# Agents' weights read from PSUM, top-k words and ranks kept in a PSUM bank, key maxima taken in PSUM by halves

## The chip, the cores and the metric

The kernel runs on one core of a Trainium2 chip. The metric is the device time of one execution in microseconds; lower is better. Three runs of the kernel before gave 364.14, 364.25 and 367.25 us, median 364.25.

The names of the engines in the rows are PE (TensorE's matmuls), PEld (its weight loads), DVE (VectorE), ACT (ScalarE), POOL (GpSimd) and SP (the engine that issues most DMAs).

## What is computed

Agent attention over 4 batches of 12608 tokens with 128 channels and 49 agents, and behind it an expert of one hidden layer for the 128 tokens of each batch that score highest.

```python
def sm(a, b):
    s = scale * (a @ b.transpose(0, 2, 1))
    s = s - s.max(-1, keepdims=True)
    e = np.exp(s)
    return e / (e.sum(-1, keepdims=True) + 1e-09)
agent_v = sm(agents, k) @ v
x = sm(q, agents) @ agent_v
...
scores = np.einsum('bsd,d->bs', x, w_gate)
out = x.copy()
for b in range(B):
    top_idx = np.argpartition(-scores[b], capacity)[:capacity]
    xe = x[b, top_idx]
    ye = np.maximum(xe @ w1, 0.0) @ w2
    g = 1.0 / (1.0 + np.exp(-scores[b, top_idx]))
    out[b, top_idx] = x[b, top_idx] + g[:, None] * ye
```

## The kernel before

Each batch is cut into 7 chunks, six of 15 tiles of 128 tokens and one of 9. Queries and keys arrive transposed, one DMA of 960 KB a chunk (576 KB for the short one), values in another; five buffers in SBUF take turns for all of them and, later, for the output.

**Scores** (`scores`, L205). For one chunk of keys or queries TensorE makes two halves, of 32 agents each. A half is four matmuls that put 32 partitions each into one PSUM bank `S`; four tokens' columns lie side by side over the 128 partitions. There are two such banks (`psS`, shared with a part of the output matmuls at the end). VectorE transposes each half in 32 x 32 blocks into SBUF (L220), so that tokens lie on partitions, with the tile and the agent along the row.

**Key side.** `k_front` (L229) takes, after both halves, the maximum over the chunk's tiles for each agent (L238, a strided reduction of 735 elements to 49). `k_max` (L242) reduces over chunks, then over partitions by a transpose on TensorE, and spreads the 49 maxima over all partitions by a matmul with a diagonal. POOL subtracts them (L264), ScalarE takes the exponent (L267), and TensorE accumulates with the values into the bank `av` (L282).

**Agents' weights** (`v_finish`, L290). A matmul adds the two halves of `av` into `pw` in PSUM. VectorE divides by the sum of exponents (L302), takes each agent's product with the gate's weights as a further column (L303), finds a power of two that scales the whole into range (`iv`, L312 and L315), scales (L320), and splits the scaled 129 columns into a 16-bit high part `ws[:, 0]` (L323) and low part `ws[:, 1]` (L324).

**Query side.** Scores, maxima (L340), subtraction on POOL (L347), exponent on ScalarE (L348), and a split into two 16-bit parts (L368, L373), which TensorE transposes (L392). The gate's scores `pg` come from 396 matmuls of three columns (L407), which need `ws`, the outputs `po` from 792 (L448). Most of the outputs are made after all input is loaded, in the order of batches 0, 1, 3, 2; ScalarE, VectorE and POOL bring them to SBUF (L455 to L467), POOL multiplying for batches 3 and 2, and SP stores them.

**Top-k** (`topk`, L506). For each batch the 128 x 99 gate scores become integer words that sort like the numbers (L518 to L530). `radix` (L478) finds the word that bounds the top 128 in two searches of 8 rounds, on the high and then on the low half-word. In a round VectorE compares all words with three bounds (L489), TensorE counts (L494), VectorE sums (L496) and moves the bound (L500). Then ranks are made by prefix sums (L549 to L559), and two matmuls (L569) turn ranks into a list of tokens. The counts, the high half-words and the counting matmuls use a bank of PSUM: `R` for batches 0, 1 and 2, which therefore take turns (a list, `counting`, also keeps the program text in that order), and `V` for batch 3. A search's words lie in SBUF.

**Experts** (`expert`, L616). POOL gathers the 128 rows by an indirect DMA (L633), queries for batches 0 to 2, which are then attended anew (`attend`), stored outputs for batch 3. TensorE transposes them (`qT`, L642) and makes the hidden layer (`ph`, L664) and the result (`py`, L676); POOL scatters it over the stored outputs (L686). The last two scatters end the kernel.

**What sets the order.** The program is written as generators that are advanced beside the main loop, with priorities (TOPK, RANK, CHASE, GATES and others). A scheduler then lays the instructions of each engine in one fixed order, by dependencies, priorities and its own estimates of durations. Each engine runs its row in that order, so an instruction that waits holds up all that stand behind it.

## Time and profile before

| | |
|---|---|
| runs | 364.14, 364.25, 367.25 us |
| profiled execution | 367.46 us, its span from first to last instruction 365.2 us |
| busy share of the span | PE 84%, DVE 79%, POOL 50%, ACT 46% |
| granted TensorE clock, mean | 0.932 |
| HBM | 79.83 MB read, 26.21 MB written |
| chain of waits, by engine | PE 52%, DVE 32%, POOL 5%, issue 4%, DMA 4%, ACT 2% |

Spans are read from the first instruction. A busy share is a mean over stretches with different limits; which engine limits a stretch is read from the table of stretches and from the idle times in the timelines. An entry of a timeline may hold several instructions of one line (x8), with the duration of all. Matmuls of fp32 data appear twice in it, once for each pass.

### The profile page before, as it was taken

Reading aid. Unit: us, or ns where it says so; the run is one execution under the profiler, and the core shown is the slowest. Engines: PE = TensorE matmul, PEld = TensorE weight load, DVE = VectorE, ACT = ScalarE, POOL = GpSimd, SP = SyncE. Lnnn points to the kernel's source line nnn. Section 1 sums busy time; section 2 is a strip of 40 time slices with the busy share of each in tenths; the row PEclk is TensorE's granted clock in tenths of the full one; section 3 lists DMA queues with packets and bytes.
Section 4 is the critical chain, followed back from the end, with each engine's and each line's share of the span. In section 5 each row is a group of like instructions: output and inputs, shape, how many; then the busy total and the mean of one; then the engine's idle time right before and its main releaser. Section 6 shows DMA issues by size and latency. Waiting matters only on the chain.

```text
span 365.2 us, 9066 instructions
## 1 busy us (share of the span) xinstructions
PE 308.0 (84%) x3669; PEld 199.9 (55%) x3669; DVE 287.6 (79%) x761; ACT 169.6 (46%) x293; POOL 182.9 (50%) x149
## 2 busy tenths in 40 slices
...
GB/s 298 408 420 415 346 281 391 228 304 334 420 377 132 367 359 336 347 385 141 396 337 308 403 354 178 157 189 222 2 263 293 351 286 209 305 355 257 133 375 16
DMA packets 18586, 106.63 MB, mean 292 GB/s; under 512 B 2544, under 2 KB 3952, under 8 KB 18544
## 3 DMA queue, kind: packets, MB, share of 16 engines
...
q8 instruction: 29, 0.48, 0.5%
q0 software_dynamic: 256, 0.52, 0.4%
...
HBM read 79.83 MB, written 26.21 MB: 290 GB/s over the span
## 4 chain that ended last, share of the span: by engine, by line
PE 52%; DVE 32%; POOL 5%; issue 4%; DMA 4%; ACT 2%; POOLq 0%; ACTq 0%; DVEq 0%
PE S L213 17%; PE po L448 10%; PE av L282 9%; PE fT L392 6%; DVE mx L238 6%; DVE sk L220 5%; DVE sq L220 3%; PE pg L407 3%; DVE qm L340 2%; PE bk L494 2%; DMA cst<-consts 2%; DVE qm L351 2%; POOL sq L347 2%; DMA out<-og 1%; POOL f L373 1%
## 5 line engine op out<-in xcount | busy, mean ns | idle before, releaser
L213 PE MATMUL S<-xT,ag_sb 128*32 128x480 f32 (+1 forms) x896 | 117.0, 586 | 15.2 <-DMA ag_sb<-agT 6.3
L393 ACT COPY ft<-fT 98x896 f16<-98x896 f16 (+2 forms) x49 | 42.7, 899 | 58.4 <-PE fT L392 58.2
L448 PE MATMUL po<-ws,ft 98*128 98x128 f16 x792 | 63.7, 235 | 5.8 <-DVE ws L323 2.2
L347 POOL TENSOR_TENSOR sq<-sq,qm 128x735 f32<-128x735 f32 (+1 forms) x28 | 38.2, 1369 | 56.6 <-DVE qm L340 52.3
L448 PEld LDWEIGHTS <-ft 98*128 98x128 f16 x792 | 54.8, 107 | 14.2 <-issue 13.4
L282 PE MATMUL av<-v,sk 128*64 128x129 f32 x792 | 60.9, 291 | 0.6 <-ACT sk L267 0.6
L213 PEld LDWEIGHTS S<-xT,ag_sb 128*32 128x32 f32 x896 | 24.9, 113 | 61.5 <-issue 16.8
L282 PEld LDWEIGHTS av<-v,sk 128*64 128x64 f32 x792 | 50.2, 144 | 11.5 <-issue 7.5
L373 POOL TENSOR_TENSOR f<-sq,f 128x735 f16<-128x735 f32 (+1 forms) x28 | 41.2, 1476 | 28.7 <-ACT f L368 23.7
L264 POOL TENSOR_TENSOR sk<-sk,mb 128x735 f32<-128x735 f32 (+1 forms) x28 | 46.7, 1712 | 10.0 <-DVE mb L257 10.0
L220 DVE STREAM_TRANSPOSE sk<-S 128x480 f32<-128x480 f32 (+1 forms) x56 | 35.0, 640 | 12.0 <-PE S L213 11.2
L348 ACT ACTIVATE sq<-sq,lift 128x735 f32<-128x735 f32 (+1 forms) x28 | 24.8, 887 | 41.0 <-POOL sq L347 40.8
L392 PEld LDWEIGHTS <-f 128*98 128x98 f16 x396 | 26.9, 127 | 23.0 <-issue 16.4
L238 DVE TENSOR_REDUCE mx<-sk 128x49 f32<-128x735 f32 (+1 forms) x28 | 38.9, 1390 | 0.3
L392 PE MATMUL fT<-idh,f 128*98 128x128 f16 x396 | 34.1, 227 | 5.4 <-POOL f L373 4.5
L220 DVE STREAM_TRANSPOSE sq<-S 128x480 f32<-128x480 f32 (+1 forms) x56 | 34.7, 636 | 5.0 <-PE S L213 4.7
L368 ACT CAST f<-sq 128x735 f16<-128x735 f32 (+1 forms) x28 | 22.0, 789 | 31.2 <-POOL sq L362 24.5
L362 POOL TENSOR_TENSOR sq<-sq,qm 128x735 f32<-128x735 f32 (+1 forms) x14 | 19.1, 1367 | 31.7 <-DVE qm L355 28.2
L467 POOL TENSOR_TENSOR og<-og,r 128x512 f32<-128x512 f32 (+2 forms) x33 | 30.3, 946 | 7.6 <-ACT og L466 5.0
L496 DVE TENSOR_REDUCE bk<-bk 128x3 f32<-128x99 f32 x64 | 16.5, 259 | 21.1 <-PE bk L494 20.6
L457 ACT ACTIVATE og<-po,iv 128x512 f32<-128x512 f32 (+1 forms) x35 | 22.3, 669 | 20.6 <-PE po L448 13.4
L267 ACT ACTIVATE sk<-sk 128x735 f32<-128x735 f32 (+1 forms) x28 | 22.1, 797 | 18.7 <-POOL sk L264 18.2
...
## 6 DMA issues: line engine op xcount, KB each, us to landing
...
```

The source lines that it names most:

```text
L213: nc.tensor.matmul(ps[32 * i:32 * i + 32, :w], ag_sb[:, b, 32 * h:32 * h + 32], xt[:, w * i:w * i + w], start=True, stop=True,)
L220: nc.vector.transpose(dst[:, :n, 32 * h:32 * h + 32], ps[:, :w].rearrange("p (t c) -> p t c", c=32),)
L238: nc.vector.tensor_reduce(d["mx"][:, c], s[:, :n, :A].rearrange("p t a -> p a t"), axis=AX.X, op=ALU.max)
L264: nc.gpsimd.tensor_tensor(sv, sv, st[b]["mb"].unsqueeze(1).broadcast_to([P, n, A]), op=ALU.subtract)
L282: nc.tensor.matmul(d["av"][o:o + AP_, :C + 1], d["S"][c][:, t], d["v", c][:, t], start=(j < 2), stop=(j >= COLS - 2),)
L347: nc.gpsimd.tensor_tensor(sv, sv, m[:, :n].unsqueeze(2).broadcast_to([P, n, A]), op=ALU.subtract)
L348: nc.scalar.activation(sv, sv, AF.Exp, scale=SCALE, bias=lift)
L373: nc.gpsimd.tensor_tensor(f[:, :n, A:], st[b]["q", c][:, :n, :A], f[:, :n, :A], op=ALU.subtract)
L392: nc.tensor.transpose(pt[:2 * A, P * t:P * t + P], f[:, t0 + t, :], idh)
L393: (nc.vector.tensor_copy if TURN[b][t0 // 8] == "V" else nc.scalar.copy)(d["ft", c][:2 * A, P * t0:P * (t0 + nt)], pt[:2 * A, :P * nt])
L448: nc.tensor.matmul(p3[:, t], q_tile(b, c, t0 + t), d["W"][:, i, :C], start=(i == 0), stop=(i == 1))
L467: nc.gpsimd.tensor_tensor(o4, o4, rate.broadcast_to([P, nt, C]), op=ALU.mult)
```

## The change

Three parts. *Key maxima*: the reduction moves into `scores`. Right after each half's transpose VectorE reduces the same PSUM bank along its row, 480 elements to 1, one maximum for each of the 128 partitions; `k_max` then works on 2 columns instead of 49. *Agents' weights*: the high and low parts are made from `pw` in PSUM by one operation each, with the reciprocal sum and the scale as per-partition factors; the 129th column and the factors' product go to ScalarE (four small operations) and POOL (one subtraction). *Top-k*: the scores are first copied into the search's PSUM bank, and the words, half-words, comparisons and ranks are written there, at four places (0, KEYS, SUMS, FREE) that are used again in turn; ScalarE copies two constants that VectorE copied or read before.

```diff
-    def scores(src, b, c, dst):
+    def scores(src, b, c, dst, top=None):
...
             nc.vector.transpose(
                 dst[:, :n, 32 * h:32 * h + 32],
                 ps[:, :w].rearrange("p (t c) -> p t c", c=32),
             )
+            if top is not None:
+                nc.vector.tensor_reduce(top[:, h:h + 1], ps[:, :w], axis=AX.X, op=ALU.max)
...
-        scores(kT, b, c, s)
+        scores(kT, b, c, s, d["mx"][:, c])
         d["S"][c] = s
-        nc.vector.tensor_reduce(
-            d["mx"][:, c], s[:, :n, :A].rearrange("p t a -> p a t"), axis=AX.X, op=ALU.max
-        )
...
-        nc.vector.tensor_reduce(m2, pt[:A, :P], axis=AX.X, op=ALU.max)
-        dg = sm.tile([P, A], F32, tag="m1", name=f"dg_{b}", bufs=1)[:A]
-        nc.vector.tensor_scalar(dg, idf[:A, :A], m2, None, op0=ALU.mult)
+            m2, pt[:2, :P].rearrange("h (i a) -> h a i", a=32), axis=AX.X, op=ALU.max
+        )
+        dg = sm.tile([2, 2, 32], F32, tag="dg", name=f"dg_{b}", bufs=1)
...
-        wsc = a[:R]
-        nc.vector.tensor_scalar(wsc, wf[:, :C + 1], iv[:R, 1:2], None, op0=ALU.mult)
+        up = iv[:R, 1:2]
         ws = sm.tile([R, 3, C + 1], F16, tag="ws", name=f"ws_{b}", bufs=B)
         nc.gpsimd.memset(ws[:, 2, C:], 1.0)
-        nc.vector.tensor_copy(ws[:, 0], wsc)
-        nc.vector.tensor_tensor(ws[:, 1], wsc, ws[:, 0], op=ALU.subtract)
-        nc.vector.tensor_scalar(
-            iv[:, 0:1], iv[:, 0:1], 2.0 ** -WEXP / FSCALE, None, op0=ALU.mult
-        )
+        nc.vector.tensor_scalar(ws[:, 0, :C], pw[:R, :C], rs, up, op0=ALU.mult, op1=ALU.mult)
+        g2 = sm.tile([R, 2], F32, tag="g2", name=f"g2_{b}", bufs=1)
+        nc.scalar.mul(g2[:, 0:1], rs, up)
+        nc.scalar.mul(g2[:, 1:2], wf[:, C:C + 1], up)
+        nc.vector.scalar_tensor_tensor(
+            ws[:, 1, :C], pw[:R, :C], g2[:, 0:1], ws[:, 0, :C], op0=ALU.mult, op1=ALU.subtract
+        )
+        nc.scalar.copy(ws[:, 0, C:], g2[:, 1:2])
+        nc.gpsimd.tensor_tensor(ws[:, 1, C:], g2[:, 1:2], ws[:, 0, C:], op=ALU.subtract)
+        nc.scalar.mul(iv[:, 0:1], iv[:, 0:1], 2.0 ** -WEXP / FSCALE)
...
-        si = sc.bitcast(I32)
-        key = t("key", "ka", dt=I32)
+        hi, key, half, sb = (bk[:, x:x + COLS] for x in (0, KEYS, SUMS, FREE))
+        nc.vector.tensor_copy(sb, sc)
+        si, key, half = sb.bitcast(I32), key.bitcast(I32), half.bitcast(I32)
+        k1 = t("k1", "ka", dt=I32)
...
-        nc.vector.tensor_tensor(key, key, si, op=ALU.bitwise_xor)
-        hii = t("hii", "kb", dt=I32)
-        nc.vector.tensor_scalar(hii, key, 16, 65535, op0=ALU.arith_shift_right, op1=ALU.bitwise_and)
+        nc.vector.tensor_tensor(key, k1, si, op=ALU.bitwise_xor)
+        nc.vector.tensor_scalar(half, key, 16, 65535, op0=ALU.arith_shift_right, op1=ALU.bitwise_and)
...
-        gt = t("gt", "kb")
-        eq = t("eq", "kd")
+        gt, eq = bk[:, :COLS], bk[:, FREE:FREE + COLS]
...
-        rank = t("rank", "ka")
+        rank = bk[:, KEYS:KEYS + COLS]
+        rk = t("rk", "ka")
...
-        nc.vector.tensor_copy(pos[:, COLS:], cs("prow"))
+        nc.scalar.copy(pos[:, COLS:], cs("prow"))
...
-        nc.vector.tensor_tensor(bs[:, 2:4], bs[:, 0:2], cn, op=ALU.add)
-        nc.vector.scalar_tensor_tensor(rank, rank, bs[:, 0:1], gt, op0=ALU.add, op1=ALU.mult)
+        nc.vector.tensor_tensor(bs[:, 2:4], pe_[:, 0:2], cn, op=ALU.add)
+        nc.vector.scalar_tensor_tensor(rank, rk, bs[:, 0:1], gt, op0=ALU.add, op1=ALU.mult)
...
-            srow = cs("srow")[:, P * i:P * i + P]
+            srow = bk[:, :P]
+            nc.scalar.copy(srow, cs("srow")[:, P * i:P * i + P])
```

The scheduler's rows change with it, all through the program. Three places follow; the numbers in a tile's name are batch and chunk (for `S` the half too, for `po` the first tile), then the buffer.

VectorE's row at the first key chunks of batch 0, before:

```order
L220 STREAM_TRANSPOSE sk_0_1_138<-S_0_1_0_141 128x15x32
L220 STREAM_TRANSPOSE sk_0_1_138<-S_0_1_1_147 128x15x32
L238 TENSOR_REDUCE mx_0_121<-sk_0_1_138 128x49
L220 STREAM_TRANSPOSE sk_0_2_154<-S_0_2_0_157 128x15x32
L220 STREAM_TRANSPOSE sk_0_2_154<-S_0_2_1_163 128x15x32
L238 TENSOR_REDUCE mx_0_121<-sk_0_2_154 128x49
```

and now:

```order
L220 STREAM_TRANSPOSE sk_0_1_139<-S_0_1_0_142 128x15x32
L225 TENSOR_REDUCE mx_0_121<-S_0_1_0_142 128x1
L220 STREAM_TRANSPOSE sk_0_1_139<-S_0_1_1_149 128x15x32
L225 TENSOR_REDUCE mx_0_121<-S_0_1_1_149 128x1
L220 STREAM_TRANSPOSE sk_0_2_156<-S_0_2_0_159 128x15x32
L225 TENSOR_REDUCE mx_0_121<-S_0_2_0_159 128x1
```

A reduction now stands between the two transposes of a chunk, and it reads the bank that the transpose ahead of it reads.

TensorE's row where the first counting matmul of batch 2's search (`bk_2`) stands, before, among outputs of batches 0 and 1:

```order
L448 MATMUL po_1_0_4_3977<-ws_1_1777,ft_1_0_858 128x128
L448 LDWEIGHTS ft_0_5_638
L448 MATMUL po_0_5_12_3946<-ws_0_904,ft_0_5_638 128x128
L494 LDWEIGHTS ones_b_111
L494 MATMUL bk_2_2801<-jk_hi_2_0_2816,ones_b_111 128x99
```

and now, among outputs of batch 3:

```order
L456 LDWEIGHTS ft_3_1_3013
L456 MATMUL po_3_1_4_4367<-ws_3_3297,ft_3_1_3013 128x128
L502 LDWEIGHTS ones_b_111
L502 MATMUL bk_2_2837<-jk_hi_2_0_2851,ones_b_111 128x99
L502 LDWEIGHTS ones_b_111
```

The search of batch 2 has moved behind all outputs of batch 1 and the first six groups of batch 3's.

The end of TensorE's row, before, from the last output matmul (the transposes `qT_2` and `qT_3` and the rank matmuls L569 stand further up, among the outputs):

```order
L448 MATMUL po_2_6_0_4905<-ws_2_2551,ft_2_6_2722 128x128
L602 MATMUL eT_2_0_3975<-idf_102,e_2_0_3958 49x128
L607 MATMUL xx_2_0_3989<-eT_2_0_3987,wfs_119 128x128
L608 MATMUL xx_2_0_3989<-wfs_119,eT_2_0_3987 128x129
L664 MATMUL ph0_3_0_4628<-xT_3_0_4607,w1_held_3464 128x128 x2
```

and now, from the same place (L577 is the rank matmul, L650 the transpose):

```order
L456 MATMUL po_2_6_8_4965<-ws_2_2582,ft_2_6_2758 128x128
L550 LDWEIGHTS tri_b_113
L550 MATMUL bk_2_2837<-cn_2_3160,tri_b_113 128x2
L551 LDWEIGHTS ones_b_111
L551 MATMUL bk_2_2837<-cn_2_3160,ones_b_111 128x1
L577 MATMUL bk_2_2837<-pos_2_3166,p1_2_0_3177 128x100 x2
L577 MATMUL bk_3_3474<-pos_3_3869,p1_3_0_3880 128x100 x2
L650 MATMUL qT_2_0_3966<-idf_102,xq_2_0_3765 128x128
```

The last steps of both searches and the start of both experts have moved behind the last output matmul. POOL's row ends accordingly, now:

```order
L475 TENSOR_TENSOR og_2_5_4892<-og_2_5_4892,r_2_2829 128x384
L475 TENSOR_TENSOR og_2_6_4940<-og_2_6_4940,r_2_2829 128x512
L641 DMA xq_2_0_3765<-q2,idx_2_0_3191 128x128
L641 DMA xq_3_0_4614<-out3,idx_3_0_3906 128x128
L694 DMA out2<-ye_2_0_4109,idx_2_0_3191 12672x128
L694 DMA out3<-ye_3_0_4722,idx_3_0_3906 12672x128
```

where the two gathers (L633 before) stood 9 and 6 products earlier.

## Rows read from the trace of the kernel before

**Rows 1.** The table of stretches: busy time of each engine in microseconds and, in brackets, its instructions, then the granted TensorE clock, the mean busy share of the DMA engines, and GB/s.

```profile
10.00:47.00 37.00, 27.25 (x256) 8.36 (x248) 36.80 (x58) 8.48 (x10) 17.89 (x12) 1.00 0.97 391
47.00:220.00 173.00, 152.18 (x1837) 86.27 (x1835) 153.29 (x339) 77.36 (x97) 105.87 (x73) 0.96 0.88 326
...
303.00:350.00 47.00, 38.35 (x504) 36.03 (x501) 34.79 (x141) 37.65 (x118) 32.07 (x35) 0.85 0.66 267
350.00:365.20 15.20, 8.65 (x68) 7.89 (x68) 4.45 (x14) 1.08 (x6) 3.21 (x4) 0.94 0.38 154
```

**Rows 2.** The timeline of VectorE from 335 to 343 us: start, duration, engine, line, operation, output<-input, shapes, count, and in square brackets the idle time before it.

```profile
336.31 2.74 DVE L554 TENSOR_TENSOR bs<-bs,cn 128x2 f32<-128x2 f32 x1
338.98 0.31 DVE L555 SCALAR_TENSOR_TENSOR rank<-rank,bs,gt 128x99 f32<-128x99 f32 x1
...
339.44 0.47 DVE L565 TENSOR_SCALAR p<-cst,bs 128x128 f32<-128x128 f32 x2
...
342.17 0.15 DVE L579 CAST idx<-ji 128x1 uint32<-128x1 f32 x1
```

**Rows 3.** The timeline of POOL from 330 to 362 us, with the same columns.

```profile
335.19 0.99 POOL L633 DMA_INDIRECT xq<-q,idx  x1 [4.40 <-DVE js_lo L500]
336.20 2.83 POOL L467 TENSOR_TENSOR og<-og,r 128x384 f32<-128x384 f32 x3
343.12 0.99 POOL L633 DMA_INDIRECT xq<-out,idx  x1 [4.09 <-PE po L448]
```

**Rows 4.** VectorE's instructions grouped by line and shape over the whole span, those that make the agents' weights: busy microseconds and mean nanoseconds of one, then the idle time just before them.

```profile
L323 DVE CAST ws<-avs 98x129 f16<-98x129 f32 x4 | 5.1, 1286 | 0.0
...
L324 DVE TENSOR_TENSOR ws<-avs,ws 98x129 f16<-98x129 f32 x4 | 4.8, 1203 | 0.0
...
L320 DVE TENSOR_SCALAR avs<-wfs,iv 98x129 f32<-98x129 f32 x4 | 4.6, 1143 | 0.1
...
L302 DVE TENSOR_SCALAR wfs<-pw,rs 98x128 f32<-98x128 f32 x4 | 1.4, 344 | 0.0
```

**Rows 5.** The timeline of TensorE, from 40 to 160 us and from 160 to 365 us, those matmuls before which it stood idle; the square brackets hold the idle time and what ended it.

```profile
90.25 0.28 PE L247 MATMUL mT<-idf,m 128*49 128x128 f32 x1 [1.66 <-DVE m L245]
...
104.41 0.22 PE L448 MATMUL po<-ws,ft 98*128 98x128 f16 x1 [2.21 <-DVE ws L323]
106.20 2.78 PE L407 MATMUL pg<-ws,ft 98*128 98x3 f16 x99 [1.58 <-DVE ws L324]
...
220.50 0.51 PE L407 MATMUL pg<-ws,ft 98*128 98x3 f16 x14 [2.86 <-DVE ws L324]
...
247.33 0.41 PE L494 MATMUL bk<-jk_lo,ones_b 128*128 128x99 bf16 x3 [2.05 <-DVE jk_lo L489]
```

**Rows 6.** VectorE's instructions grouped by line and shape, as in the fourth group: the maxima of the keys (L238), the maxima of the queries (L340) and the sum of the counts in PSUM (L496).

```profile
L238 DVE TENSOR_REDUCE mx<-sk 128x49 f32<-128x735 f32 x24 | 35.2, 1468 | 0.2
...
L340 DVE TENSOR_REDUCE qm<-sq 128x15 f32<-128x735 f32 x24 | 21.6, 902 | 0.2
...
L496 DVE TENSOR_REDUCE bk<-bk 128x3 f32<-128x99 f32 x64 | 16.5, 259 | 21.1 <-PE bk L494 20.6
...
L340 DVE TENSOR_REDUCE qm<-sq 128x9 f32<-128x441 f32 x4 | 2.4, 598 | 0.0
```

**Rows 7.** The timeline of all engines from 198 to 262 us, two entries of the score matmuls: a chunk's sixteen (two passes of eight) one behind the other, and a single one (two passes) between other matmuls.

```profile
209.59 1.82 PE L213 MATMUL S<-xT,ag_sb 128*32 128x480 f32 x16
...
235.15 0.99 PE L213 MATMUL S<-xT,ag_sb 128*32 128x480 f32 x2
```

**Rows 8.** ScalarE's instructions from 303 to 350 us grouped by line and shape, the one of a single column.

```profile
L655 ACT ACTIVATE g<-xe 128x1 f32<-128x1 f32 x1 | 0.2, 206 | 0.0
```

**Rows 9.** VectorE's instructions grouped by line and shape, as in the fourth group: those that make the words of the top-k search.

```profile
L521 DVE TENSOR_TENSOR key<-key,sc 128x99 int32<-128x99 int32 x4 | 4.5, 1130 | 0.0
...
L518 DVE TENSOR_SCALAR key<-sc 128x99 int32<-128x99 int32 x4 | 2.6, 641 | 0.0
...
L525 DVE CAST bk<-hii 128x99 f32<-128x99 int32 x4 | 1.0, 258 | 0.0
...
L523 DVE TENSOR_SCALAR hii<-key 128x99 int32<-128x99 int32 x4 | 0.8, 206 | 0.0
```

**Rows 10.** The timeline of TensorE from 341 to 361 us: the transpose of batch 2's gathered rows, and the last output matmuls.

```profile
345.21 0.42 PE L642 MATMUL qT<-idf,xq 128*128 128x128 f32 x1
...
348.99 0.61 PE L448 MATMUL po<-ws,ft 98*128 98x128 f16 x8 [0.36 <-ACT og L466]
```

**Rows 11.** The timeline of all engines from 320 to 344 us: the starts of two rounds of a search, the index of batch 2, and the rank matmuls of batch 3.

```profile
320.05 0.53 DVE L489 SCALAR_TENSOR_TENSOR jk_lo<-bk,sp_lo,cst 128x297 bf16<-128x297 f32 x1
...
321.16 0.53 DVE L489 SCALAR_TENSOR_TENSOR jk_lo<-bk,sp_lo,cst 128x297 bf16<-128x297 f32 x1
...
334.76 0.15 DVE L579 CAST idx<-ji 128x1 uint32<-128x1 f32 x1
...
340.40 1.18 PE L569 MATMUL bk<-pos,p 128*128 128x100 f32 x4 [2.44 <-DVE p L566]
```

**Rows 12.** The DMA issues from 330 to 366 us: transfer, queue, count, size where it is known, and the microseconds from issue to landing.

```profile
xq<-q,idx POOLq DMA_INDIRECT x1, 5.5
xq<-out,idx POOLq DMA_INDIRECT x1, 2.5
```

**Rows 13.** VectorE's instructions from 303 to 350 us grouped by line and shape, the sum of the counts, one for each round of a search.

```profile
L496 DVE TENSOR_REDUCE bk<-bk 128x3 f32<-128x99 f32 x19 | 4.9, 264 | 1.8 <-PE bk L494 1.6
```

34 lines of the change are left out of this document (18 added, 16 removed).

## The prediction

> **What bounds the kernel now.** The table of stretches comes first [rows 1]. From 10 to 47 us VectorE is busy for 36.80 of 37.00 us and the DMA share is 0.97: key chunks pass through it one after the other. From 47 to 220 us TensorE (152.18 of 173.00) and VectorE (153.29) are both near 88%. From 303 to 350 us, where the output tiles of batches 3 and 2 are made, TensorE (38.35 of 47.00), ScalarE (37.65) and VectorE (34.79) stand close together. The last 15.20 us hold TensorE for 8.65 and VectorE for 4.45: a chain of small steps, the experts of batches 2 and 3.
>
> **The stalls that the change touches.** Next, single rows. Some VectorE operations are slow for what they do: L554 adds two columns and took 2.74 us from 336.31 [rows 2]; POOL's products span 336.20 to 339.03 [rows 3], and both end together. L323 casts 129 columns in 1.29 us on average, L324 subtracts in 1.20, while L302, with about as many columns read from PSUM, takes 0.34 [rows 4]. So operations with all their data in SBUF wait for POOL, and those with a PSUM operand mostly don't. TensorE's idle time behind such operations is in its timeline [rows 5]: 1.66 us for the reduction of the maxima, 2.21 and 1.58 for batch 0's weights, 2.86 for batch 2's, 2.05 behind the keys of batch 2. Together 10.4 us; that is what TensorE could get back before 303 us.
>
> **The change, part by part.**
>
> *Key maxima.* A reduction of 735 elements (1468 ns, 24 times) gives way to two of 480 straight from PSUM [rows 6]; the four short chunks I take as unchanged. The contiguous reductions of L340 give the slope, (902 - 598) / (735 - 441) = 1.03 ns an element, so 480 elements cost 902 - 255 x 1.03 = 639 ns. L496 reads PSUM: 259 ns for 99 elements where that line gives 245, so 14 ns more, 653 ns. A chunk goes from 1.47 to 1.31 us, 24 x 0.16 = 3.9 us in all. The price is elsewhere: each of the two PSUM banks of scores is now held 0.65 us longer before TensorE may refill it (first order rows: transpose, reduction, transpose, reduction). A half of the scores takes TensorE 0.91 us, 1.82 for two [rows 7], so after a key chunk the next second half comes some 0.5 us late if nothing stands between. I credit half of the 3.9, 2 us, mostly before 47 us; bounds nothing and 3.9.
>
> *The maxima's chain* (L245, L252) shrinks from 49 rows to 2; of the 1.66 us gap [rows 5] I take 0.5, and as much for the batches behind it twice, 1.5 us.
>
> *Weights.* L320, L323 and L324 took 1143 + 1286 + 1203 ns = 3.63 us [rows 4]. Now there are two PSUM operations like L302, 0.34 each, and between them a ScalarE product for which VectorE waits: a one-column activation, 0.21 us [rows 8], plus what stands ahead of it in ScalarE's queue, which I bound by nothing and by the 1.3 us of the cast that it replaces; I take 0.5. Behind the waiting operation stand score transposes, and TensorE's banks with them. TensorE's share is what it waited: of batch 0's 3.8 us 2.4, of batch 2's 2.86 all, because other matmuls now stand ahead of the gate. The gate's second column goes through POOL's queue; I charge 1 us for that (nothing to 2).
>
> *Top-k words.* L518 and L521 took 641 and 1130 ns, the other four some 0.2 each, 2.6 us [rows 9]. With a PSUM operand each should cost what L525 does, 258 ns, and a copy is added: 7 x 0.258 = 1.8 us. Of the 2.05 us gap I take 1.5. The Trainium skill speaks against this step: "VectorE: DVE Perf Modes", section Why PSUM operands drop a tier, says that a PSUM operand bars the two-port mode, and its Rules for kernel authors advise to copy PSUM to SBUF first if many operations follow. The trace agrees for undisturbed ones, L523 at 206 ns against L525 at 258 [rows 9]. By that rule alone this part costs some 52 ns more for each of seven operations, 0.4 us a search, and gains nothing.
>
> *Ranks.* L554 falls back from 2.74 us [rows 2] to a small step; this counts in the last stretch, below.
>
> *The order.* The scheduler places everything anew. Score matmuls of one half run four at a time only when they are adjacent: alone one takes 0.99 us, as long as a half [rows 7]. The order before breaks such groups 12 times, after 15 times: 3 x 0.8 = 2.4 us lost, less what is done between; 1.5.
>
> Before 303 us the sum is 2 + 1.5 + 2.4 + 2.86 + 1.5 - 1 - 1.5 = 7.8 us gained; I take 6.5, since a gap that closes in one queue often opens in the next.
>
> *The end.* This decides. The searches of batches 0, 1 and 2 follow each other in one bank. With the gate of batch 0 later and the words kept in that bank, search 2 begins among batch 3's outputs instead of batch 1's (second order rows), and searches 2 and 3 run to the very end: the rank matmuls of both stand behind the last output matmul, the gathers behind POOL's last product (third). Before, the last output matmul ended at 349.6 us [rows 10], when both gathers were long done (issued at 335.19 and 343.12, [rows 3]), and the end came 365.2 - 349.6 = 15.6 us later. After, behind the last output matmul at T: count matmuls, 0.3; five steps of offsets and ranks at 0.23 (two between 338.98 and 339.44, [rows 2]) and four of slots at about as much, 2.1; rank matmuls, 0.5; index, 0.9; from the index to POOL's gather 0.3 (334.91 to 335.19, [rows 3, 11]). Gather at T + 4.1. It lands after 2.5 to 5.5 us [rows 12]; 4.0, since the last stores still drain. qT_2 at T + 8.1. From qT_2 to the end it was 365.2 - 345.2 = 20.0 us [rows 10]; without output work between I take 1.2 off, 18.8. So the end is T + 26.9, 11.3 us worse (8.5 to 13.5).
>
> From 303 us to T there are 32 rounds of search instead of 19 [rows 13]. A round takes 1.11 us from start to start (320.05 to 321.16, [rows 11]) and 0.3 of TensorE: VectorE 34.8 + 14 + 2 for one more prologue, less some 8 for stalls and epilogues, 43 of 47 us; TensorE 38.4 + 4 = 42. Covered by each other, so nothing (-4 to +4).
>
> **The sum.** T moves by -6.5, the tail by +11.3: +4.8 us. The profiled execution took 367.46 us, of them 365.2 in its span; the runs have a median of 364.25. The difference goes onto the median: 369 us.
>
> **Rivals.**
>
> *The relief is worth more.* All five gaps go (10.4), the key maxima give 3.9, and TensorE's wait for the rank operations at 340.40 (2.44, [rows 11]) and one like it before fall, 4.5: 18.8 less 11.3 is 7.5 us gained, 357 us. For it: VectorE and TensorE are both near 88% from 47 to 220 us. Against: TensorE has only 21 us free there. It decides when T comes over 15 us earlier.
>
> *Gain and tail cancel.* T earlier by 8 to 15 us: 361 to 368 us.
>
> *The banks and the last searches bind.* Score banks held longer stop TensorE, 0.5 us at some 14 changes from a key to a query chunk, 7 us, so that only the weights' relief is left, or two full searches push T by 4 us: 373 to 377 us. The same comes out if the slow operations do not get faster from PSUM, the change then not doing what it says.
>
> **How the numbers follow.** Forecast 0.36, banks and searches 0.12, cancelling 0.30, relief 0.22. A measurement of this kernel can tell about 1%, 3.6 us. So slower 0.48, same 0.30, faster 0.22. The likeliest case alone spans 368 to 373 us; the range reaches into the others on both sides, 358 to 376.
>
> **What would show it.** Right: the last output matmul at about 343 us of the span, the gathers of batches 2 and 3 behind it, and some 27 us from there to the end; reductions from PSUM near 0.65 us; the weights' two operations near 0.34. Wrong: T over 10 us earlier, a gather that lands in 2.5 us, output work that outlasts the searches, or score matmuls that wait for the reductions.

## The result and the profile after

The changed kernel has a median of 352.61 us (352.18 to 356.64, four runs) beside 364.41 us for the kernel before on the same chip: ratio 0.9684, 95% interval 0.9599 to 0.9769. It is faster by 3.2%; 369 us was forecast, and the range from 358 us up misses it. The profiled execution has a span of 350.9 us, 14.3 less, and a mean granted clock of 0.959 where it was 0.932. A kernel can also run in a slower state with a lower granted clock; the ratios are of runs outside it, and the one profile below that was taken in it (before_all_held) is not read.

The table of stretches of the kernel after, with the columns of [rows 1]:

```profile
10.00:47.00 37.00, 29.13 (x260) 8.17 (x256) 35.67 (x65) 10.14 (x12) 19.66 (x13) 1.00 0.96 390
47.00:220.00 173.00, 160.51 (x2031) 94.28 (x2023) 136.49 (x347) 83.43 (x116) 114.27 (x82) 0.97 0.92 352
...
0.00:318.50 318.50, 288.12 (x3586) 179.05 (x3587) 250.57 (x735) 168.89 (x309) 177.79 (x148) 0.98 0.85 328
318.50:350.90 32.40, 15.95 (x84) 13.16 (x82) 11.88 (x47) 2.52 (x11) 5.51 (x6) 0.72 0.17 67
```

And of the kernel before, from the start to its last output matmul:

```profile
0.00:349.60 349.60, 299.24 (x3601) 191.98 (x3601) 282.88 (x747) 168.11 (x287) 179.26 (x146) 0.93 0.79 298
```

The last output matmul ends at T = 318.5 us instead of 349.6, 31.1 us earlier. Up to it TensorE is idle for 318.50 - 288.12 = 30.4 us, before 349.60 - 299.24 = 50.4. VectorE is busy 32 us less up to there, of which 7 have moved behind T (11.88 us after; 4.45 in the last row of [rows 1]). Behind it, in the tail, the kernel needs 32.4 us instead of 15.6, at a granted clock of 0.72.

From 47 to 220 us VectorE fell from 153.29 [rows 1] to 136.49 us and TensorE rose from 152.18 to 160.51: the same stretch now holds more of the work.

VectorE's groups by shape, beside [rows 4, 6, 9]:

```profile
L225 DVE TENSOR_REDUCE mx<-S 128x1 f32<-128x480 f32 x48 | 29.7, 618 | 0.0
...
L326 DVE TENSOR_SCALAR ws<-pw,rs,iv 98x128 f16<-98x128 f32 x4 | 1.6, 402 | 0.0
L330 DVE SCALAR_TENSOR_TENSOR ws<-pw,g,ws 98x128 f16<-98x128 f32 x4 | 1.4, 354 | 0.6 <-ACT g L328 0.5
...
L531 DVE TENSOR_TENSOR bk<-k,bk 128x99 int32<-128x99 int32 x4 | 1.0, 259 | 0.0
...
L528 DVE TENSOR_SCALAR k<-bk 128x99 int32<-128x99 int32 x4 | 1.0, 257 | 0.1
...
L561 DVE TENSOR_TENSOR bs<-bk,cn 128x2 f32<-128x2 f32 x4 | 0.6, 148 | 0.0
```

A reduction from PSUM takes 618 ns (653 forecast), the weights' two operations 402 and 354 (344), the words 0.26 each (0.258). The wait for ScalarE ahead of the weights' second operation is 0.5 us for all four batches; I had taken 0.5 for each. The addition of two columns (L561), which took 2.74 us beside POOL's products [rows 2, 3], takes 0.15.

TensorE's timeline, beside [rows 5]: the transpose of batch 0's maxima and the first gate matmuls of batch 2, with the idle time ahead of them:

```profile
84.45 0.27 PE L246 MATMUL mT<-idf,m 128*2 128x128 f32 x1 [0.81 <-DVE m L244]
...
210.92 1.52 PE L415 MATMUL pg<-ws,ft 98*128 98x3 f16 x52 [1.75 <-POOL ws L334]
```

The wait for the maxima halved from 1.66. Batch 2's gate, which waited 2.86 us for VectorE, now waits 1.75 for the one subtraction that went to POOL's queue; I had charged 1 us for it.

The end, in the timeline of all engines, beside [rows 3, 10]: batch 2's first rank matmul, a step that waits for it, and the second; the gather and the transpose of batch 2, the same of batch 3, the hidden layer, the last scatter:

```profile
321.89 0.49 PE L577 MATMUL bk<-pos,p 128*128 128x100 f32 x2 [2.97 <-DVE p L574]
...
322.42 0.35 DVE L573 TENSOR_SCALAR p<-bk,bs 128x128 f32<-128x128 f32 x1 [0.58 <-PE bk L577]
...
323.21 0.75 PE L577 MATMUL bk<-pos,p 128*128 128x100 f32 x2 [0.83 <-DVE p L574]
...
325.37 1.00 POOL L641 DMA_INDIRECT xq<-q,idx  x1 [4.34 <-DVE idx L587]
...
327.92 0.48 PE L650 MATMUL qT<-idf,xq 128*128 128x128 f32 x1 [0.69 <-DMA xq<-q,idx]
...
329.58 0.96 POOL L641 DMA_INDIRECT xq<-out,idx  x1 [3.21 <-PE sc L598]
...
332.17 0.45 PE L650 MATMUL qT<-idf,xq 128*128 128x128 f32 x1 [2.72 <-DMA xq<-out,idx]
...
335.01 3.36 PE L672 MATMUL ph<-xT,w_held 128*128 128x128 f32 x14 [0.58 <-DVE xT L653]
...
347.20 0.98 POOL L694 DMA_INDIRECT out<-ye,idx  x1 [0.79 <-DVE ye L687]
```

and the hidden layer of the kernel before:

```profile
351.38 1.83 PE L664 MATMUL ph<-xT,w_held 128*128 128x128 f32 x14 [0.58 <-DVE xT L645]
```

The order at the end is the one forecast: rank matmuls and both gathers behind the last output.

**One account for all kernels.** The time to T is split in three for TensorE. *Idle* is T less the busy time of the row from 0 to T. *Lost to the clock* is the sum, over stretches of 1 us, of the busy time times (1 - granted clock). *Work* is the busy time less that, as if at full clock. Before: 50.4 idle, 21.5 lost, 277.7 work. After: 30.4, 5.1, 283.0. Of the 31.1 us, 20.0 are idle time and 16.4 the clock, and work rose by 5.3. What is lost to the clock is an upper bound, since not all matmuls get shorter at full clock (shown below).

### The profile page after: what moved, and what is told of

The parts are those of the page before. It is cut to its first block, busy times and chain, and to the rows that moved or that the text cites. A ratio compares the mean times of both kernels' runs of the same rounds, so it can differ in the third digit from the quotient of the medians.

```text
span 350.9 us, 9140 instructions
## 1 busy us (share of the span) xinstructions
PE 304.1 (87%) x3669; PEld 192.2 (55%) x3669; DVE 262.4 (75%) x781; ACT 171.4 (49%) x317; POOL 183.3 (52%) x153
## 5 line engine op out<-in xcount | busy, mean ns | idle before, releaser
L213 PE MATMUL S<-xT,ag_sb 128*32 128x480 f32 (+1 forms) x896 | 119.0, 572 | 16.3 <-DMA ag_sb<-agT 6.2
L456 PE MATMUL po<-ws,ft 98*128 98x128 f16 x792 | 57.1, 220 | 3.4 <-ACT og L472 1.7
L286 PE MATMUL av<-v,sk 128*64 128x129 f32 x792 | 58.2, 281 | 0.6 <-ACT sk L271 0.6
L213 PEld LDWEIGHTS S<-xT,ag_sb 128*32 128x32 f32 x896 | 24.1, 110 | 61.7 <-issue 25.2
L286 PEld LDWEIGHTS av<-v,sk 128*64 128x64 f32 x792 | 47.6, 138 | 12.2 <-issue 7.3
L456 PEld LDWEIGHTS <-ft 98*128 98x128 f16 x792 | 48.4, 98 | 8.7 <-issue 7.5
L220 DVE STREAM_TRANSPOSE sq<-S 128x480 f32<-128x480 f32 (+1 forms) x56 | 35.7, 644 | 18.2 <-PE S L213 14.1
L220 DVE STREAM_TRANSPOSE sk<-S 128x480 f32<-128x480 f32 (+1 forms) x56 | 35.9, 641 | 13.5 <-PE S L213 13.5
L376 ACT CAST f<-sq 128x735 f16<-128x735 f32 (+1 forms) x28 | 22.0, 789 | 30.3 <-POOL sq L370 15.4
L475 POOL TENSOR_TENSOR og<-og,r 128x512 f32<-128x512 f32 (+2 forms) x33 | 30.4, 942 | 6.8 <-POOL og L475 3.9
L225 DVE TENSOR_REDUCE mx<-S 128x1 f32<-128x480 f32 (+1 forms) x56 | 33.0, 590 | 0.0
L504 DVE TENSOR_REDUCE bk<-bk 128x3 f32<-128x99 f32 x64 | 16.8, 262 | 13.4 <-PE bk L502 12.2
L472 ACT ACTIVATE og<-po,r 128x128 f32<-128x128 f32 x81 | 25.9, 497 | 1.4 <-PE po L456 1.4
```

Source lines behind the costliest of these rows:

```text
L213: nc.tensor.matmul(ps[32 * i:32 * i + 32, :w], ag_sb[:, b, 32 * h:32 * h + 32], xt[:, w * i:w * i + w], start=True, stop=True,)
L220: nc.vector.transpose(dst[:, :n, 32 * h:32 * h + 32], ps[:, :w].rearrange("p (t c) -> p t c", c=32),)
L225: nc.vector.tensor_reduce(top[:, h:h + 1], ps[:, :w], axis=AX.X, op=ALU.max)
L286: nc.tensor.matmul(d["av"][o:o + AP_, :C + 1], d["S"][c][:, t], d["v", c][:, t], start=(j < 2), stop=(j >= COLS - 2),)
L456: nc.tensor.matmul(p3[:, t], q_tile(b, c, t0 + t), d["W"][:, i, :C], start=(i == 0), stop=(i == 1))
L472: nc.scalar.activation(o4[:, t], p3[:, t], AF.Copy, scale=rate[:, t])
```

## The experiments

My theory after the result: the gaps cost more than their length, because the clock falls behind them, and the new rows (the scheduler's orders) matter as much as the faster operations. Rivals: the operations do it all; or the rows do it all. A kernel said to have *held rows* keeps the order of every engine as recorded, by edges of order alone; in the others the scheduler lays its own rows. No kernel leaves out computation; where products are added, nobody reads them. Every ratio is to the kernel before on the same chip; the account is that of the profiled execution. T and the tail are single measurements, so differences of a microsecond or two between them are weak.

| kernel | rows | ratio (95%) | T | tail | idle | lost to clock | work |
|---|---|---|---|---|---|---|---|
| before | | 1 | 349.6 | 15.6 | 50.4 | 21.5 | 277.7 |
| after | | 0.9684 (0.9599 to 0.9769) | 318.5 | 32.4 | 30.4 | 5.1 | 283.0 |
| keys_only | own | 0.9647 (0.9608 to 0.9687) | 331.6 | 22.5 | 44.1 | 11.2 | 276.3 |
| topk_only | own | 0.9646 (0.9593 to 0.9699) | 326.6 | 28.7 | 42.0 | 19.4 | 265.2 |
| weights_only | own | 1.0391 (1.0334 to 1.0447) | 360.3 | 22.8 | 40.4 | 20.1 | 299.8 |
| before_filled | before's | 0.9876 (0.9812 to 0.9941) | 342.7 | 20.1 | 41.3 | 8.5 | 292.9 |
| before_keys_held | before's | 0.9935 (0.9889 to 0.9982) | 350.3 | 15.7 | 49.4 | 22.5 | 278.4 |
| before_topk_held | before's | 0.9886 (0.9836 to 0.9936) | 345.0 | 20.0 | 47.8 | 19.6 | 277.6 |
| before_weights_held | before's | 1.0194 (1.0124 to 1.0264) | 355.2 | 17.2 | 52.0 | 25.7 | 277.5 |
| before_all_held | before's | 0.9895 (0.9839 to 0.995) | – | – | – | – | – |
| after_ws_sbuf | after's | 0.9834 (0.974 to 0.9928) | 325.6 | 32.5 | 35.0 | 8.2 | 282.4 |
| after_words_sbuf | after's | 0.9712 (0.9677 to 0.9747) | 322.7 | 34.0 | 34.7 | 4.9 | 283.1 |
| after_keys_sbuf | after's | 0.9717 (0.9663 to 0.9771) | 320.3 | 32.6 | 32.5 | 6.5 | 281.3 |
| after_all_sbuf | after's | 1.0046 (1.0007 to 1.0085) | 334.7 | 33.4 | 45.7 | 7.1 | 281.9 |
| before_joined | before's, joined | 0.9849 (0.9807 to 0.9891) | 344.3 | 15.7 | 50.8 | 28.8 | 264.8 |
| weights_joined | weights_only's, joined | 0.9837 (0.977 to 0.9904) | 335.2 | 21.0 | 43.8 | 11.6 | 279.8 |
| after_joined | after's, joined | 0.9518 (0.9412 to 0.9625) | 310.1 | 32.1 | 34.5 | 6.7 | 268.9 |
| after_warm | after's, filled | 0.9759 (0.9669 to 0.9849) | 319.4 | 34.1 | 30.7 | 6.7 | 282.0 |
| joined_more | joined further | 0.934 (0.9304 to 0.9377) | 308.7 | 32.5 | 33.9 | 6.7 | 268.1 |
| joined_warm | the same, filled | 0.9262 (0.9199 to 0.9324) | 308.0 | 30.2 | 33.1 | 6.6 | 268.3 |

### One part alone, own rows

keys_only, weights_only and topk_only each make one part of the change's diff on the kernel before.

> Only the key maxima are changed, weights and top-k as before; the scheduler lays its own rows. [...] Rival 'VectorE time' (the gain is in proportion to the work taken from VectorE; 9.0 of 30 us are the maxima's, of 12 us gained): 3.6 us, 361 us. Rival 'order' (the new rows as a whole carry the gain, no part does alone): 364 us or above.

> Only the agents' weights are changed. Theory 'clock': the gaps of 3.8 us (batch 0) and 2.86 us (batch 2) close and the low clock behind them (6.8 and 10.2 us at 0.5) goes, 6.7 + 8.5 us in TensorE's row, of which the later searches give some back: 7 to 12 us gained, 352 to 357 us, no granted clock under 0.9 between 100 and 115 us nor between 220 and 231. Rival 'VectorE time' (13.1 of 30 us): 5.3 us gained, 359 us, wherever the clock stands. Rival 'order': 364 us or above.

> Only the words and ranks of the top-k search are changed. Theory 'clock': gaps of 2.05, 2.04, 2.08 and 2.44 us close, 3.4 + 6.8 + 6.8 us of low clock behind them go, but both last searches end behind the outputs (the rank products of batch 3 stand behind the last output product), so the tail eats most of it: 2 to 6 us gained, 358 to 362 us. Rival 'VectorE time' (7.9 of 30 us): 3.2 us gained, 361 us. Rival 'order': 364 us or above.

Measured: 3.5% faster, 3.9% slower, 3.5% faster. The theory 'clock', that a closed stop gives back itself and a part of the low clock behind it, had 360 to 363, 352 to 357 and 358 to 362 us, that is 0.3 to 1.2%, 2.0 to 3.4% and 0.6 to 1.7% below 364.25, and misses all three. Not every stop has a low clock behind it, either: in the kernel before, the clock stays at 1.00 behind stops of 1.66 us at 90.25 and of 1.79 at 37.73, and it is 0.57 from 281 to 289 us with no stop over 0.3 us in the ten us ahead, but with 99 gate matmuls of three columns between 275.9 and 280.3. The parts do not add up to the whole (by the ratios -13, +14 and -13 us of 365, against -12 for all), so a sum over parts, as in the prediction, cannot hold: each edit has the scheduler lay all rows anew. weights_only makes the same faster operations and has 10 us less idle time than before, but 22 us more work; it breaks the score groups 24 times, the kernel before 12 times. All score matmuls together hold TensorE for 128.6 us there, for 117.0 in the kernel before, 112.0 in keys_only and 108.2 in topk_only, so a part of each swing is how they stand in the row (see below).

### The stops filled, nothing else changed

before_filled holds the rows of before and puts some 220 unread products ahead of eight matmuls that wait for VectorE or POOL.

```diff
+    def busy(n, into, by, first):
...
+        made = []
+        for _ in range(n):
+            made.append(by(into).ins)
+        ins = first().ins
...
+        fill["ahead"][ins.name] = made
...
+            if c == t == 0 and b in (0, 2):
+                busy(18 if b == 0 else 34, d["spare"], plain, go)
```

> The kernel before with every engine's row kept as it is; only, where TensorE stood idle behind slow VectorE or POOL work (61.02, 104.41, 106.20, 220.50, 247.33, 327.85, 331.36 and 340.40 us), 18 to 50 small products that nobody reads fill some 85% of the wait. VectorE does exactly what it did, as slowly as it did. Theory 'clock': the granted clock stays near 1.0 behind the filled waits; 17.8 us were lost to the low clock there, about half to two thirds of it reaches the end, 352 to 357 us. Rival 'VectorE time' and rival 'stall' (only the wait itself costs; the low clock behind it lies beside VectorE's work): 362 to 366 us.

The table of stretches from 220 to 231 us, behind the stop of 2.86 us [rows 5], of the kernel before:

```profile
220.00:231.00 11.00, 10.49 (x146) 9.30 (x145) 5.58 (x17) 5.61 (x7) 8.64 (x7) 0.53 0.48 176
```

of before_filled:

```profile
220.00:231.00 11.00, 10.58 (x177) 7.85 (x176) 5.49 (x17) 5.61 (x7) 8.57 (x7) 1.00 0.61 208
```

and of the kernel after:

```profile
220.00:231.00 11.00, 11.00 (x75) 4.11 (x72) 2.08 (x6) 4.77 (x6) 1.53 (x1) 1.00 0.57 199
```

TensorE runs near 1.2 GHz (0.53) for 11 us behind that stop, and at 2.4 GHz when the stop is filled. So this stop costs clock beyond its own length. What the clock does to single matmuls is in the same stretch, value and gate matmuls of the kernel before:

```profile
221.67 3.70 PE L282 MATMUL av<-v,sk 128*64 128x129 f32 x30
225.30 0.96 PE L407 MATMUL pg<-ws,ft 98*128 98x3 f16 x30
```

and of before_filled:

```profile
221.47 1.97 PE L298 MATMUL av<-v,sk 128*64 128x129 f32 x30
223.37 0.95 PE L428 MATMUL pg<-ws,ft 98*128 98x3 f16 x30
```

Thirty value matmuls take half the time at 1.00, thirty gate matmuls of three columns the same time. The worth at the end is smaller than the sum: 13 us less are lost to the clock, T comes 6.9 us earlier, the end 1.2%. The account says where the rest is. Of the 15.2 us more of work, 12.9 are the unread products themselves, 3.8 more than the 9.1 us of idle time that they fill; the other 2.3 are time booked as lost to the clock that full clock does not give back. So the clock gives T some 10.7 us of the 13.0 (an estimate, 6.9 + 3.8), and 4.5 us go again in the tail (20.1 us instead of 15.6, granted clock 0.75 there). New stretches of low clock open near 158 and 274 us. By its ratio it would take 359.7 us where the kernel before takes 364.25, between the theory's 352 to 357 and the rivals' 362 to 366, and so misses both.

### The operations alone, in before's rows

The four held kernels put one part, or all, into the rows of before. In before_weights_held and before_all_held VectorE makes the whole of the weights, with one-column operations of its own instead of ScalarE's and POOL's.

```diff
+        nc.vector.tensor_tensor(g2[:, 0:1], rs, up, op=ALU.mult)
+        nc.vector.tensor_tensor(g2[:, 1:2], wf[:, C:C + 1], up, op=ALU.mult)
+        nc.vector.tensor_scalar(ws[:, 0, :C], pw[:R, :C], g2[:, 0:1], None, op0=ALU.mult)
```

> The operations of the key maxima as after, but every engine's row kept as in the kernel before (the new reductions stand right behind their transposes). Theory 'operations' (shorter VectorE work and closed stalls carry the gain, whatever the rows): 4 to 7 us gained, ratio 0.981 to 0.989. Rival 'rows' (what the scheduler lays anew carries the gain of 13 us that this part showed by itself): ratio 0.99 to 1.01.

> The agents' weights made straight from PSUM, all of it on VectorE (no step through ScalarE or POOL), every engine's row kept as in the kernel before. Theory 'operations': TensorE's waits of 3.8 us (batch 0) and 2.86 us (batch 2) close to under 1 us each and part of the low clock behind them goes: 6 to 10 us gained, ratio 0.973 to 0.984; the 14 us that this part lost by itself were then its rows'. Rival 'the operations themselves cost' (PSUM operands hold the banks): ratio 1.00 or above, as by itself.

> Words and ranks of the top-k search in the PSUM bank, the two constants still on VectorE or in SBUF, every engine's row kept as in the kernel before but for the words of batches 1 and 2, which now stand behind their bank's first instruction. Theory 'operations': the waits of 2.05, 2.04, 2.08 and 2.44 us close, 4 to 8 us gained, ratio 0.978 to 0.989. Rival 'rows': ratio 0.99 to 1.01.

> The three parts together in the rows of the kernel before, so that the tail keeps its old form (both gathers hidden, 15 to 20 us behind the last output product). Theory 'operations': the parts add up to 14 to 22 us, ratio 0.94 to 0.96, below the changed kernel's 0.968. Rival 'rows': ratio 0.98 or above, the changed kernel's gain needs its rows.

Keys 0.65% and top-k 1.1% faster, weights 1.9% slower, all three together 1% faster: keys and the whole come out as the rival 'rows' had it, top-k at the upper end of what the theory 'operations' wanted. VectorE's groups by shape in before_weights_held:

```profile
L324 DVE TENSOR_TENSOR g<-wfs,iv 98x1 f32<-98x1 f32 x4 | 5.6, 1398 | 0.0
...
L323 DVE TENSOR_TENSOR g<-rs,iv 98x1 f32<-98x1 f32 x4 | 3.3, 834 | 0.1
...
L325 DVE TENSOR_SCALAR ws<-pw,g 98x128 f16<-98x128 f32 x4 | 1.4, 341 | 0.0
```

A product of one column with all its data in SBUF takes up to four times as long as one of 128 columns that reads PSUM. The stall that the change removes came back in my substitute, so its 1.9% says nothing about the change's own weights, and before_all_held carries the same stall. The change's real weights in before's rows were not tried.

### The data put back into SBUF, in after's rows

The other side of the cross: the rows and the list of operations of after, with one part's data in SBUF.

```diff
-        nc.vector.tensor_scalar(ws[:, 0, :C], pw[:R, :C], rs, up, op0=ALU.mult, op1=ALU.mult)
+        nc.vector.tensor_scalar(ws[:, 0, :C], wf[:, :C], up, None, op0=ALU.mult)
...
-                nc.vector.tensor_reduce(top[:, h:h + 1], ps[:, :w], axis=AX.X, op=ALU.max)
+                nc.vector.tensor_reduce(top[:, h:h + 1], dst[:, :n, 32 * h:32 * h + 32], axis=AX.XY, op=ALU.max)
...
-        hi, key, half, sb = (bk[:, x:x + COLS] for x in (0, KEYS, SUMS, FREE))
+        hi, key, half, sb = bk[:, :COLS], own("key", "wa"), None, own("sb", "wb")
```

> The changed kernel in its own rows, number and form of instructions unchanged; only the two large operations that make the agents' weights take the normalised rows from SBUF instead of PSUM. Theory 'POOL' (a VectorE operation with all its data in SBUF stands still while POOL works, one with an operand in PSUM doesn't): they go from 402 and 354 ns to 1.0 us or more on average, and TensorE stops again ahead of the outputs or the gate; 1 to 5 us lost against the changed kernel, ratio 0.97 to 0.985. Rival 'place of the operand does not matter': 0.35 to 0.45 us each, ratio 0.965 to 0.97.

> The changed kernel in its own rows; the two reductions of a key chunk read the transposed half in SBUF instead of the PSUM bank, 480 elements as before. Theory 'POOL stalls additions and casts, not reductions' (L340 reads SBUF alone and keeps its 902 ns while POOL works): 0.60 to 0.70 us each, the bank free 0.6 us sooner, ratio 0.962 to 0.972. Rival 'every VectorE operation with all its data in SBUF waits for POOL': 0.8 us or more each, ratio 0.975 to 0.99.

> The changed kernel in its own rows; only the words and ranks of the search have their data in SBUF (all but the second scan's input and one constant), weights and key maxima as after. Theory 'POOL': the words of batch 2 meet POOL's row of key subtractions and cost 1.2 to 1.8 us each, TensorE's counting products wait; with 1.5% for the weights and under 0.5% for the maxima, what is left of the 3.7% between 0.968 and 1.0046 falls to the words: ratio 0.98 to 0.99. Rival 'the parts only hurt together': ratio 0.965 to 0.975.

> The changed kernel in its own rows, number of instructions unchanged; the weights' two large operations, the key maxima and the words and ranks of the search (all but the second scan's input and one constant) have their data in SBUF again. With the rows of after and the places of before it fills the fourth corner of the square (rows of before: 1.00 with its operations, 0.9895 with the new ones; rows of after: 0.968 with the new ones). Theory 'rows first' (most of the gain is the rows', and lets shorter operations count): ratio 0.975 to 0.99. Rival 'operations in these rows' (the rows alone give nothing): ratio 0.995 to 1.01.

VectorE's groups in after_ws_sbuf:

```profile
L326 DVE TENSOR_SCALAR ws<-wfs,iv 98x128 f16<-98x128 f32 x4 | 6.0, 1502 | 0.0
...
L330 DVE SCALAR_TENSOR_TENSOR ws<-wfs,iv,ws 98x128 f16<-98x128 f32 x4 | 4.2, 1043 | 0.0
```

two of these four L326 in the timeline, the first beside POOL's products, the last while POOL stood idle:

```profile
97.01 1.67 DVE L326 TENSOR_SCALAR ws<-wfs,iv 98x128 f16<-98x128 f32 x1
...
261.99 0.28 DVE L326 TENSOR_SCALAR ws<-wfs,iv 98x128 f16<-98x128 f32 x1
```

and in after_keys_sbuf:

```profile
L225 DVE TENSOR_REDUCE mx<-sk 128x1 f32<-128x480 f32 x48 | 31.3, 653 | 1.6
```

The weights' two operations take 1502 - 402 + 1043 - 354 = 1789 ns longer a batch, 7.2 us for four, and T is 7.1 us later. The two numbers agree, but by the account only 4.6 of the 7.1 are idle time and 3.1 are the clock, behind new stops of 2.77 us at 162.3 and 2.71 at 213.4; so it isn't shown that each microsecond of the stall is on the path. The words move T by 4.2 us, the keys by 1.8 (56 reductions at some 35 ns make 2.0). All three together move it by 16.2, 3.1 more than the single ones add up to, and the gain over before is gone (ratio 1.0046). At the end the words alone (0.9712) and the keys alone (0.9717) can't be told from after (0.9684); for the words the rival 'only hurt together' is the one that came true, and for all three the rival 'the rows alone give nothing'.

What the stall looks like, in the timeline of all engines, batch 2's words and weights. After:

```profile
196.69 9.85 POOL L268 TENSOR_TENSOR sk<-sk,mb 128x735 f32<-128x735 f32 x6
...
199.89 0.26 DVE L528 TENSOR_SCALAR k<-bk 128x99 int32<-128x99 int32 x1
...
200.18 0.27 DVE L531 TENSOR_TENSOR bk<-k,bk 128x99 int32<-128x99 int32 x1
...
200.66 0.40 DVE L326 TENSOR_SCALAR ws<-pw,rs,iv 98x128 f16<-98x128 f32 x1
...
201.29 0.36 DVE L330 SCALAR_TENSOR_TENSOR ws<-pw,g,ws 98x128 f16<-98x128 f32 x1
```

after_all_sbuf, the same steps (L531, L534, L326, L330), and what follows them:

```profile
203.46 9.84 POOL L268 TENSOR_TENSOR sk<-sk,mb 128x735 f32<-128x735 f32 x6
...
207.09 1.71 DVE L531 TENSOR_SCALAR k<-sb 128x99 int32<-128x99 int32 x1
...
208.83 1.75 DVE L534 TENSOR_TENSOR key<-k,sb 128x99 int32<-128x99 int32 x1
...
212.20 1.18 DVE L326 TENSOR_SCALAR ws<-wfs,iv 98x128 f16<-98x128 f32 x1
...
213.47 1.38 DVE L330 SCALAR_TENSOR_TENSOR ws<-wfs,iv,ws 98x128 f16<-98x128 f32 x1
...
217.02 5.11 DVE L541 TENSOR_SCALAR lo<-half 128x99 f32<-128x99 int32 x1
219.04 3.02 POOL L381 TENSOR_TENSOR f<-sq,f 128x735 f16<-128x735 f32 x2
...
222.20 0.43 PE L502 MATMUL bk<-jk_hi,ones_b 128*128 128x99 bf16 x3 [11.16 <-DVE jk_hi L497]
```

Both rows run beside POOL's products. With data in PSUM each VectorE step takes 0.26 to 0.40 us; with data in SBUF 1.18 to 1.75, about one POOL product (9.84 / 6 = 1.64), and one of 99 elements took 5.11 and ended with POOL's products at 222.1. With the same data in SBUF but POOL at rest, L326 took 0.28 us (261.99 above), less than the 0.40 from PSUM: POOL makes the delay, not SBUF. TensorE's queue stands behind the row of these steps: 11.16 us idle. The Trainium skill, "SBUF — State Buffer", section Who interferes with whom, says that operations with two SBUF inputs and the two-port modes contend with POOL and that reductions never do on this chip. The reductions agree: 653 ns on average from SBUF, 618 from PSUM, and none of the 56 took over 654.

The account of after_all_sbuf cuts the change in two. From before to it (new rows, new list of operations, data in SBUF): idle 4.7 less, lost to the clock 14.4 less, work 4.2 more, T 14.9 earlier, the tail 17.8 longer, the end no earlier. From it to after (the data's place alone): idle 15.3 less, clock 2.0 less, work 1.1 more, T 16.2 earlier, the tail 1.0 shorter, the end 3.6% earlier (0.9684 / 1.0046 = 0.964). So the new rows bring most of the clock and the data's place most of the idle time, and at the end neither gives the gain alone as far as it was tried: the rows with data in SBUF 0.5% slower, the operations in the old rows 1% faster, with weights that stall.

### Adjacent score matmuls

The *joined* kernels hold the rows of before, weights_only or after with one thing moved: the four matmuls of a score half stand one behind the other. In TensorE's row of after_joined against after:

```diff
 L415 MATMUL pg_2667<-ws_2582,ft_5_2510 128x3
-L213 MATMUL S_4_0_3105<-xT_4_3103,ag_sb 32x480
-L415 LDWEIGHTS ft_5_2510
-L415 MATMUL pg_2667<-ws_2582,ft_5_2510 128x3
-L213 MATMUL S_4_0_3105<-xT_4_3103,ag_sb 32x480
...
+L213 MATMUL S_4_0_3105<-xT_4_3103,ag_sb 32x480 x4
 L415 LDWEIGHTS ft_5_2510
 L415 MATMUL pg_2667<-ws_2582,ft_5_2510 128x3
```

> The kernel before, nothing of the change in it, in its own rows; only the score products of the 5 halves that stand apart (12 breaks) are moved up behind their first. Theory 'adjacency': the score products go from 117 to about 105 us of TensorE, and 5 to 10 us reach the end, ratio 0.973 to 0.986. Rival 'slack': ratio 0.993 to 1.0.

> Only the agents' weights changed, in the rows that the scheduler gave that kernel, but the score products of a half that stand apart (11 halves, 24 breaks) moved up behind their first. Theory 'adjacency': the score products go from 128.6 to about 108 us, 10 to 18 us gained against the 14 us that this part lost, ratio 0.99 to 1.01. Rival 'the operations cost' (steps through ScalarE and POOL): ratio 1.03 or above, as it was.

> The changed kernel in its own rows, but the score products of a half that stand apart (8 of 112 halves, 15 breaks) are moved up behind their first. Theory 'adjacency' (apart, each takes TensorE about as long as four together): the score products go from 119 to about 107 us of TensorE, the last output product comes 6 to 12 us earlier, the later searches give back up to half: 3 to 8 us gained, ratio 0.945 to 0.96. Rival 'slack' (TensorE's own time does not set the end): under 2 us, ratio 0.963 to 0.97.

TensorE's score matmuls of whole chunks, grouped by shape, in the kernel before:

```profile
L213 PE MATMUL S<-xT,ag_sb 128*32 128x480 f32 x768 | 105.4, 615 | 14.3 <-DMA ag_sb<-agT 6.3 <-DVE sk L220 3.8 <-DVE qm L352 2.0
```

in weights_only:

```profile
L213 PE MATMUL S<-xT,ag_sb 128*32 128x480 f32 x768 | 113.6, 614 | 15.3 <-DMA ag_sb<-agT 6.2 <-DVE sk L220 3.9 <-DVE sq L220 2.7
```

in weights_joined:

```profile
L213 PE MATMUL S<-xT,ag_sb 128*32 128x480 f32 x768 | 94.8, 600 | 15.9 <-DMA ag_sb<-agT 6.1 <-DVE sk L220 4.5 <-DVE sq L220 2.6
```

in the kernel after:

```profile
L213 PE MATMUL S<-xT,ag_sb 128*32 128x480 f32 x768 | 105.3, 598 | 13.2 <-DMA ag_sb<-agT 6.2 <-PE S L213 2.5 <-DVE mx L225 2.1
```

and in after_joined:

```profile
L213 PE MATMUL S<-xT,ag_sb 128*32 128x480 f32 x768 | 95.1, 595 | 14.4 <-DMA ag_sb<-agT 6.2 <-DVE mx L225 3.1 <-PE S L213 1.9
```

The mean of one hardly moves; the busy time, in which four overlap or don't, falls by 18.8 and 10.2 us. With the short chunks' it falls from 128.6 to 105.3 us for 24 breaks (0.97 us each), from 119.0 to 105.5 for 15 (0.90) and, in before_joined, from 117.0 to 104.1 for 12 (1.08). That turns weights_only from 3.9% slower into 1.6% faster, and the changed kernel gains another 1.7% (by 0.9518 with an interval of 1.1% either way). The kernel before gains 1.5% by it: its work falls by 12.9 us, but 7.3 more are lost to the clock. So what made weights_only slow was the order of one engine's row, not the weights: joined, it stands beside the joined kernel before (0.9837 and 0.9849). And adjacency is not what the change as a whole gains by: joined on both sides it is still worth 3.4% (0.9518 / 0.9849 = 0.966).

### The tail warmed

after_warm holds after's rows and puts 44, 12, 9 and 40 unread products ahead of the waiting matmuls of the tail. joined_more regroups, in after_joined's row, also single transposes and gate and value matmuls by kind; joined_warm adds 8 and 24 products ahead of its two transposes `qT`, in the part of that bank that nobody reads.

```diff
         pt = pm("qT")
-        nc.tensor.transpose(pt[:, :n], xq[:n, :C], idf[:n, :n])
+        go = lambda: nc.tensor.transpose(pt[:, :n], xq[:n, :C], idf[:n, :n])
+        if b >= 2:
+            busy(8 if b == 2 else 24, pt[:, P:2 * P], plain, go)
```

> The changed kernel in its own rows; behind the last output product 105 small products that nobody reads fill TensorE's waits ahead of the rank products and of the two transposes. Theory 'clock in the tail' (17 us at a granted clock of 0.5 behind 322 us cost TensorE 4.9 us in a chain where nothing else runs): the clock stays near 1.0, 3 to 6 us gained, ratio 0.951 to 0.96. Rival 'the chain waits for VectorE and transfers': under 1.5 us, ratio 0.964 to 0.97.

> The changed kernel with the score halves joined and, where single products of three kinds (scores' transposes back, gate, values) take turns, up to 24 of them regrouped by kind: 367 runs of one kind instead of 400. By the slope of the five kernels so far (17 us of TensorE's work less from 484 to 420 runs, 18 us less from 420 to 329; 0.2 to 0.25 us a run) 7 us of work less, half of it at the end: 2 to 5 us below the joined kernel, ratio 0.938 to 0.948. Rival 'only the scores care' : ratio 0.949 to 0.957.

> The kernel with joined scores and regrouped single products, and behind the last output product 8 and 24 small products that nobody reads ahead of the two transposes of gathered rows (into banks that VectorE does not read then). Theory 'clock in the tail': the clock is back near 1.0 when the experts' first products begin, their 14 products take 1.9 us instead of 3.4: 1 to 3 us below the kernel without them, ratio 0.925 to 0.931. Rival 'chain of VectorE and transfers': ratio 0.932 to 0.938.

TensorE's timeline in after_warm, the products meant to fill the first wait:

```profile
322.74 3.83 PE L239 MATMUL bk<-ones_b 128*128 128x99 bf16 x44 [2.96 <-DVE p L589]
```

and in joined_warm, the second filling and the hidden layer:

```profile
318.74 2.76 PE L239 MATMUL qT<-ones_b 128*128 128x128 bf16 x24
...
324.37 1.83 PE L691 MATMUL ph<-xT,w_held 128*128 128x128 f32 x14 [0.58 <-DVE xT L672]
```

after_warm lost: its first 44 products go into the bank that VectorE reads, so they waited out the stop themselves (2.96 us) and then stood in the way; the tail grew from 32.4 to 34.1, though its hidden layer too takes 1.83 us. In joined_warm the products run while the gather is under way, the hidden layer's 14 matmuls take 1.83 instead of 3.36 us, and the tail is 30.2, 2.3 shorter than in joined_more. joined_more itself is 1.8% better than after_joined by the ratios, but only 1.0 us by the spans (341.2 and 342.2), on chips where the kernel before takes 368.3 and 364.8 us, and after_joined's runs lie between 343.95 and 350.38 us. Its work fell by 0.8 us where 7 were expected, so that regrouping other matmuls by kind pays is not shown.

joined_warm, median 342.09 us against 369.42 for the kernel before on its chip, is the fastest: 7.4% less than before. Its interval overlaps that of joined_more, so the tail's 2.3 us are read from the timelines, not from the ratios.

## Why the prediction was wrong

**The direction of T and of the tail was right, the sign of the sum wrong**: T by -31.1 instead of -6.5 us, the tail by +16.8 instead of +11.3. Two of the signs that I had named for being wrong came true, T over 10 us earlier and a gather that lands in 2.5 us.

*"TensorE's share is what it waited"* failed. I priced a gap at its idle time and had no term for the clock behind it. 16.4 us of T are clock, and before_filled shows in the old rows that stops bring it down: there 13.0 us of clock were worth some 10.7 at T, and 2.4 at the end after 3.8 us of surplus products and 4.5 of tail. For the change itself it isn't settled how much of the 16.4 reaches the end. With data in SBUF and the new rows (after_all_sbuf), 14.4 of the 16.4 are there already: the missing term belongs to the order, which I had priced by its breaks alone.

*The weights and words* (2.4 + 2.86 + 1.5 = 6.8 us) were mis-sized. The place of the data is worth 16.2 us of T in the new rows, nearly all idle time. I counted only gaps with a visible wait at the operation's own consumer; stalls in one queue lengthen waits elsewhere (11.16 us of TensorE behind a row of search steps and the weights, new stops ahead of counting matmuls in after_ws_sbuf). POOL's subtraction, charged 1 us, let the gate wait 1.75.

*The order* (-1.5) had nearly the right price for a break, 0.8 us where 0.90 to 1.08 was measured, and the wrong role. It isn't a small correction: the parts alone swing by 3.5% either way with their rows.

*"A gap that closes in one queue often opens in the next"* took 7.8 to 6.5, in the wrong direction: idle time fell by 20.0.

*The tail.* The gather was issued at 325.37 - 318.5 = 6.9 us behind T, not 4.1: the rank steps stand one behind the other, TensorE waits 2.97 us for the first slots, the next slots wait for that rank matmul (0.58) and the second matmul for them (0.83), where I had let slots and matmuls run through. It landed after 2.5 us, not 4.0; the DMA engines are only 9% busy from 325.37 to 327.92, the stores are through. From the transpose to the end it took 350.9 - 327.92 = 23.0 us, not 18.8, 3.0 more than before. Of these, 2.0 are the same missing term: at a granted clock of 0.57 the hidden layer's first 24 matmuls, 335.01 to 340.01, take 5.0 us, and in the kernel before 3.0. The other 1.0, and the 1.2 that I took off, lie ahead of them, above all where batch 2's next step stands in TensorE's row behind batch 3's transpose, which waits 2.72 us for its gather. joined_warm shows that 2.3 us of the tail can be had back.

*The rivals.* That the relief is worth more (T over 15 us earlier, 357 us) came nearest. Its 18.8 us are close to the 20.0 of idle time, in part by chance: the waits for the maxima (0.81 us) and the gate (1.75) did not go whole, while a wait for POOL that no sum had fell from 4.28 to 2.50 us. It lacked the clock, the extra work and 5.5 us of tail. That banks and searches bind is refuted for these rows: the score matmuls waited 13.2 us in all, 14.3 before in the same group, and the reductions stand for 2.1 of it; in keys_only, with other rows, they stand for 7.4 of 19.8 us in all. What I wrote against the relief, that TensorE had only 21 us free from 47 to 220 us, counted 6.1 us of low clock there as busy and left out what lay behind: 15.4 us lost to the clock from 220 us to T, of which nothing is left after the change.

*Open:* whether new operations alone, in the old rows, would give the whole gain. before_all_held says about 1%, but with weights that stall.
